# Where the column means of the first MLP weight are made and subtracted: first attention and its end, or five visits of the second attention

## The chip, the cores and the metric

One core of one Trainium2 chip runs the whole program. The metric is the device time of one execution in microseconds, the median of several; less is better. All arithmetic of matmuls is fp32, apart from the bucket masks in bf16.

## What is computed

The reference chains a hashed attention and an FNet block. With batch 4, 8 heads, sequence 768 and head size 64:

```python
mask = q_bucket[:, :, :, None] == k_bucket[:, :, None, :]
scores = np.where(mask, scale * np.matmul(q, k.transpose(0, 1, 3, 2)), -1e9)
attn = softmax(scores)                       # rows, with + 1e-9 below
x = (attn @ v) laid out as (B, S, H*D)       # (4, 768, 512)
mixed = np.real(fft(fft(x, axis=1), axis=2))
u = x + mixed
un = (u - mean(u)) / np.sqrt(var(u) + 1e-6)  # over the last axis
out = u + np.maximum(un @ w_ch1, 0.0) @ w_ch2
```

`w_ch1` is 512 x 2048 and `w_ch2` 2048 x 512; both arrive as 64-bit floats and are narrowed to fp32 on the core. Because `(u - mean(u)) @ w1` equals `u @ (w1 - column mean of w1)`, the kernel takes the mean out of the weight instead of out of every row: each column of `w1` has its mean over the 512 inputs subtracted once. The change is about when this is done.

## The kernel before

The batches run one after the other. `attention(b)` (from line 999) goes through 4 pairs of heads, each with 6 chunks of 128 keys: 24 steps, after each of which it yields. A step makes scores on TensorE (L909, with mask matmuls L898 for the first pairs), takes the exponential on ScalarE (L922), masks on VectorE for later pairs (L936), sums keys on VectorE (`acc`, L1041), and multiplies with v on TensorE (`oo`, L947). The exponentials have two buffers `pk`; one becomes free when its sum has been made. Beside the attention of batch b runs a second piece of work, advanced by `next(other)` between the steps: beside the first attention `weights1` (the conversion of `w1`), beside the later ones `mix(b-1)`, which is the Fourier mixing of the batch before (`cs` L1162, `A` and `B` L1191, update of x L1205) and then its MLP as Strassen products (`mlp7`: `h_p` L1471 and `o` L1350). With b = 1 also `w2` is converted on the way.

`w1` lies in SBUF as 4 row blocks by 2048 columns. `average(f)` (L659) makes the mean of 512 columns in two parts. First four matmuls with a 128 x 32 matrix of ones, one for each row block, into four 32-row bands of one PSUM bank `ws` (L664), and a ScalarE copy of that bank to the SBUF tile `part` (L669); then, after a yield, one 128 x 128 matmul with a matrix of 1/(32*512), which leaves the mean in every row of another bank, `wm` (L672). `centre(f, avg)` (L675) subtracts it from the four row blocks on VectorE (L678), 512 columns at a time. The tag `u`, which holds `part`, has two buffers; the PSUM tag `ps`, from which `ws` and `wm` come and outside the first and last stage the banks of the mixing step, has two too.

Before the change, blocks 0 and 512 are averaged and centred within `weights1`, after their fourth conversion, in the first attention. Blocks 1024 and 1536 are averaged at the end of the first attention (L1593 to L1599), their means copied to two SBUF tiles `mean` by ScalarE, and subtracted at the second step of the second attention (L1612 to L1614).

Two things set the order. Everything of the first attention and the averages at its end stands in a block whose order on all engines is that of the text (L1578). After it a planner orders each engine's instructions at compile time: among those that its cost model holds ready, the one that comes first in the text. `in_turn()` (L684) puts what it encloses behind the last recorded instruction of ScalarE and of VectorE on their queues. Centred weights are first read by `quarters` (L1257, VectorE sums L1264 to L1267 and stores `ad` of L1269 and L1270, issued by SP), which prepares the Strassen operands; `quarters(f)` reads columns f*128 and (f+8)*128. SP also issues all loads of q, k and v (L562, L568, L576).

Of the kernel before, what the change touches and what calls it, by code (L numbers as in the profile page):

```python
# [11 lines left out]
F32 = mybir.dt.float32  # L12
# [8 lines left out]
P = 128  # L21
# [3 lines left out]
DFF = 4 * DM  # L25
# [5 lines left out]
NDC = DM // P  # L31
GTT = 2
GT = GTT * P
WC = 512
# [451 lines left out]
def _main(  # L486
# [13 lines left out]
    nc = tc.nc  # L500
# [13 lines left out]
    def wt(shape, dtype, tag, name, bufs=2):  # L514
        return work.tile(shape, dtype, tag=tag, name=name, bufs=bufs)
# [4 lines left out]
    def pt(shape, name):  # L520

        turn[0] += 1
        if roomy[0] and turn[0] % 2:
            if turn[0] % 4 == 1:
                return ps_o.tile(shape, F32, tag="o", name=name)
            return ps_sc.tile(shape, F32, tag="sc", name=name)
        return ps_1.tile(shape, F32, tag="ps", name=name)
# [89 lines left out]
    mean = const.tile([P, P], F32, tag="mean", name="mean")  # L617
# [41 lines left out]
    def average(f):  # L659


        ps = pt([P, WC], f"ws{f}")
        for c in range(NDC):
            nc.tensor.matmul(  # L664
                ps[32 * c : 32 * c + 32, :], ones, w1[:, c, f : f + WC],
                start=True, stop=True,
            )
        part = wt([P, WC], F32, "u", f"part{f}", 2)
        nc.scalar.copy(part, ps)  # L669
        yield  # L670
        ps = pt([P, WC], f"wm{f}")
        nc.tensor.matmul(ps, mean, part, start=True, stop=True)  # L672
        yield ps

    def centre(f, avg):  # L675
        for c in range(NDC):
            w = w1[:, c, f : f + WC]
            nc.vector.tensor_tensor(w, w, avg, op=ALU.subtract)  # L678

    ET = mybir.EngineType  # L680
    done_by = {}

    @contextmanager
    def in_turn():  # L684

        with ExitStack() as st:
            for ins in done_by.values():
                st.enter_context(tc.issue_after(ins.ins))
            yield
# [32 lines left out]
    def weights1():  # L722
        slices = [
            (w1[:, c, f : f + WC], moe_w_ch1[c * P : (c + 1) * P, f : f + WC])
            for f in range(0, DFF, WC)
            for c in range(NDC)
        ]
        zt = wt([P, 3, 2 * WC], F32, "z", "zraw1", 1)
        ft = wt([P, 12, WC], F32, "F", "fraw", 1)
        raws = [zt[:, i] for i in range(3)] + [  # L730
            ft[:, i : i + 2].rearrange("p i w -> p (i w)") for i in range(0, 8, 2)
        ]
        arrival = Arrival(slices, raws, 0, nc.sync)
        for i in range(arrival.depth):
            arrival.fetch(i)
            if i == 2:
                load(1)
        yield
        half = None
        for i in range(len(slices)):  # L740
            arrival.convert(i, ft[:, 8 + i % 4].bitcast(I32))
            yield
            if half:
                centre(half[0], next(half[1]))
                half = None
            if i % NDC == NDC - 1:


                f = i // NDC * WC
                if f < DFF // 2:  # L750
                    half = f, average(f)
                    next(half[1])


    xs = {}
# [164 lines left out]
    def weights(pk, g, ps):  # L920

        done_by[ET.Activation] = nc.scalar.activation(  # L922
            pk[:, g, :, 0:HALF], ps[:, :, 0:HALF], AF.Exp, scale=SCALE
        )

    def weigh(n, c, pss):
# [6 lines left out]
        if kb is not None:  # L933
            for h in range(2):
                w = pk[:, :, h, 0:HALF]
                done_by[ET.DVE] = nc.vector.scalar_tensor_tensor(  # L936
                    w, qb[:, h].rearrange("p (g s) -> p g s", g=2), kb[:, h, c : c + 1], w,
# [61 lines left out]
    def attention(b):  # L999
# [14 lines left out]
        for t in range(NPAIR):  # L1014
# [12 lines left out]
            def tally(c, pk, sums):  # L1027
# [10 lines left out]
                else:  # L1038

                    for g in (0, 1) if b == 0 else (slice(0, 2),):  # L1040
                        done_by[ET.DVE] = nc.vector.tensor_tensor(  # L1041
                            acc[:, g], (first if c == 1 else acc)[:, g], new[:, g],
# [102 lines left out]
    def mix(b):  # L1145
# [8 lines left out]
        for par in range(2):  # L1154
            for t in range(NT // 2):
# [12 lines left out]
                for k in kinds:  # L1168
                    done_by[ET.Activation] = nc.scalar.copy(
                        f[:, k, k : hd + 1 - k],  # L1170
# [14 lines left out]
        for j in range(NDC):  # L1185
# [10 lines left out]
            for ps, op in (pa, ALU.add), (pb, ALU.subtract):  # L1196
                for i in range(2):
# [4 lines left out]
                    else:  # L1202
                        f = ps[:, HW : HALF + 1]
                        f = bass.AP(f.tensor, f.offset, [f.ap[0], [HW, 2], [-1, HW]])
                    done_by[ET.DVE] = nc.vector.tensor_tensor(  # L1205
                        u, u, f, op=op if (j < 2) ^ i else ALU.add
# [206 lines left out]
    def mlp7(b):  # L1413
# [66 lines left out]
        def relu(h):  # L1480
# [3 lines left out]
            else:  # L1484
                done_by[ET.Activation] = nc.scalar.activation(h, h, AF.Relu)  # L1485

# [77 lines left out]
    def after(n, one, two):  # L1564

        for i, _ in enumerate(one):
            if i >= n and (i - n) % 2 == 0:
                next(two, None)
            yield
        for _ in two:  # L1570
            pass

    other = weights1()
    next(other)

    with tc.manual_schedule(engines={ET.PE, ET.DVE, ET.Activation, ET.Pool, ET.SP}):  # L1578
        for _ in prepare(0):
            pass  # L1580
        roomy[0] = False
        for i, _ in enumerate(attention(0)):
            if i == 2 * NT - 1:
                nc.sync.dma_start(ch, cn["ch"].ap())
                nc.sync.dma_start(sq, cn["sq"].ap())
            if i % 5 < 4:
                next(other, None)
        for _ in other:
            pass
        pwf = wt([P, 2, P], F32, "ef", "pwf", 1)  # L1590
        nc.sync.dma_start(pwf, cn["pw"].ap())
        nc.scalar.copy(pw, pwf)
        means = []  # L1593
        late = [(f, average(f)) for f in range(DFF // 2, DFF, WC)]
        for _, avg in late:
            next(avg)
        for f, avg in late:
            means.append((f, wt([P, WC], F32, "u", f"mean{f}", 2)))
            nc.scalar.copy(means[-1][1], next(avg))  # L1599
    for b in range(B):  # L1600
        if b > 0:

            wait = 0
            if b == 1:
                next(other)
                next(other)
                wait = 2
            steps, done = NPAIR * NT - wait, 2 if b == 1 else 0  # L1610
            for i, _ in enumerate(attention(b), 1):
                if b == 1 and i == 2:  # L1612
                    for f, avg in means:
                        centre(f, avg)  # L1614
                while done * steps < (MIX - LEFT) * (i - wait):
                    next(other)
                    done += 1
        if b == B - 1:
            roomy[0] = True

            ms = const.tile([P, 3], F32, tag="ms", name="ms")
            nc.vector.tensor_reduce(ms[:, 0:2], norms, axis=AX.X, op=ALU.max)
            nc.vector.tensor_reduce(ms[:, 2:3], strange, axis=AX.X, op=ALU.max)
            ps = pt([1, 3, P], "norms_t")
            for io in range(3):
                nc.tensor.transpose(ps[:, io, :], ms[:, io : io + 1], ident)
            mt = const.tile([1, 5], F32, tag="mt", name="mt")
            nc.vector.tensor_reduce(mt[:, 0:3], ps, axis=AX.X, op=ALU.max)  # L1630
            nc.vector.tensor_tensor(mt[:, 3:4], mt[:, 0:1], mt[:, 1:2], op=ALU.mult)
            nc.vector.tensor_scalar(
                mt[:, 4:5], mt[:, 3:4], (SAFE / SCALE / 2) ** 2, None, op0=ALU.is_gt
            )
            fl = const.tile([1, 1], I32, tag="fl", name="fl")
            nc.vector.scalar_tensor_tensor(
                fl, mt[:, 2:3], 0.0, mt[:, 4:5], op0=ALU.is_gt, op1=ALU.max
            )
            large = nc.values_load(fl[0:1, 0:1], min_val=0, max_val=1)
        for _ in other:  # L1640
            pass
        other = mix(b)
        if b == 0:
            zt2 = wt([P, 3, 2 * WC], F32, "z", "zraw2", 1)
            arrival2 = weights2()
            other = after(NT, other, islice(arrival2, HF + 2))
# [6 lines left out]
def kernel(tc, *args):  # L1653

    cn = {n: tc.nc.inline_tensor(a, name="k_" + n) for n, a in _consts().items()}
    with ExitStack() as ctx:
        large = _main(ctx, tc, *args, cn)
    with tc.If(large > 0, preferred_fallthrough_block=True):
        _any_scores(tc, *args, cn)
# [34 lines left out]
```

## Time and profile before

| what | us |
|---|---|
| median of 3 runs | 1074.12 |
| lowest and highest | 1073.25, 1074.61 |
| the profiled execution | 1074.1 |
| its span, first to last instruction | 1072.3 |
| TensorE, weight loads, VectorE, ScalarE busy | 1033.3, 632.4, 779.6, 489.2 |
| `ws` matmuls: first and last start | 33.8, 115.2 |
| `wm` matmuls: first and last start | 39.4, 118.4 |
| subtractions from `wm`: first and last start, median of one | 40.6, 66.0, 0.680 |
| subtractions from `mean`: first and last start, median of one | 119.7, 130.6, 0.680 |
| copies to `mean`: two, median of one | 0.604 |

In the lines of the profile, a row of the chain of work has its start, its length and what ran: the engine, the tile that it writes, and the line of the code; x4 is the number of instructions merged. PE is TensorE (PEld its weight loads), DVE VectorE, ACT ScalarE, POOL GpSimd, SP the engine that issues DMAs; a q behind a name means the engine's queue. The scores matmuls of the second attention begin at 115.7 us, its mixing matmuls at 126.3 us; the third attention's begin at 394.94 us (`cs`).

### The profile page before, as it was taken

The numbers are of one execution on the slowest core, as the hardware profiler recorded it, in microseconds if no ns is written. First come the engines' busy times: TensorE is split into PE (matmuls) and PEld (weight loads), VectorE is DVE, ScalarE is ACT, GpSimd is POOL, SyncE is SP. The second block draws the span as 40 slices with busy tenths as digits, with TensorE's granted clock in tenths as the row PEclk, the third lists the DMA queues.
The fourth block names the chain that finished last, engine by engine and source line by source line (L and its number), as shares of the span: only waits on it lengthen the run. The fifth ranks groups of instructions, "written<-read, shape, count | busy, mean of one in ns | idle before, by whom it ended". The sixth has DMA issues, their size and how long they took to land.

```text
span 1072.3 us, 14129 instructions
## 1 busy us (share of the span) xinstructions
PE 1033.3 (96%) x4965; PEld 632.4 (59%) x4965; DVE 779.6 (73%) x1326; ACT 489.2 (46%) x993; POOL 59.6 (6%) x132
## 2 busy tenths in 40 slices
PE   7999899999999999999999999999999999999996
PEld 3333364457644676546665675555675579668575
DVE  5789969996799967877758877767857885644353
ACT  7888564761386323455236315354325512440420
POOL 0000000011000020100000020010000012200000
PEclk9999999999999999999999999999999999999999
DMA  8754551470154451223072242322042204223301
GB/s 207 200 143 85 112 136 45 135 233 1 35 153 150 136 194 36 45 67 81 12 200 74 66 123 88 59 64 61 15 125 86 64 25 172 65 74 100 117 20 42
DMA packets 175711, 103.13 MB, mean 96 GB/s; under 512 B 129553, under 2 KB 162961, under 8 KB 175633
## 3 DMA queue, kind: packets, MB, share of 16 engines
q1 hardware_dynamic: 169840, 88.65, 30.7%
q0 software_dynamic: 4224, 13.11, 3.9%
q8 instruction: 41, 0.67, 0.3%
q10 hardware_dynamic: 1568, 0.39, 0.2%
q14 instruction: 38, 0.30, 0.1%
HBM read 81.14 MB, written 20.97 MB: 95 GB/s over the span
## 4 chain that ended last, share of the span: by engine, by line
PE 74%; DVE 14%; ACT 5%; issue 2%; DMA 2%; SPq 1%; DVEq 0%; ACTq 0%
PE o L1350 25%; PE h_p L1471 23%; PE oo L947 9%; PE sc L909 8%; PE cs L1162 3%; DVE pk L936 2%; DVE acc L1041 2%; ACT pk L922 2%; PE A L1191 2%; PE B L1191 1%; PE sum L957 1%; DMA kn<-in_k_dram 1%; DVE x L1205 1%; PE bits L838 1%; SPq L576 1%
## 5 line engine op out<-in xcount | busy, mean ns | idle before, releaser
L1350 PE MATMUL o<-w,h 128*128 128x256 f32 x1152 | 258.6, 381 | 0.9 <-DVE w L1362 0.5
L1350 PEld LDWEIGHTS o<-w,h 128*128 128x128 f32 x1152 | 216.7, 190 | 41.6 <-issue 6.4
L922 ACT ACTIVATE pk<-sc 128x768 f32<-128x768 f32 x192 | 147.4, 808 | 78.6 <-PE oo L947 35.5
L1471 PE MATMUL h_p<-x,w 128*128 128x384 f32 x448 | 164.5, 494 | 2.4 <-ACT w L1538 1.7
L936 DVE SCALAR_TENSOR_TENSOR pk<-qb,kb,pk 128x768 f32<-128x768 bf16 x132 | 128.8, 1012 | 39.4 <-ACT pk L922 39.3
L909 PE MATMUL sc<-qt,kt 64*128 64x384 f32 x768 | 153.6, 503 | 1.6 <-ACT pk L922 1.4
L947 PE MATMUL oo<-pk,vn 128*64 128x385 f32 (+1 forms) x768 | 146.2, 495 | 1.5 <-DVE pk L936 1.3
L1471 PEld LDWEIGHTS h_p<-x,w 128*128 128x128 f32 x448 | 81.9, 190 | 68.3 <-issue 9.3
L1471 PE MATMUL h_p<-w 128*128 128x384 f32 x288 | 105.9, 489 | 0.0
L1041 DVE TENSOR_TENSOR acc<-acc,pk 128x1536 f32<-128x1536 f32 (+1 forms) x64 | 98.5, 1550 | 5.4 <-ACT pk L922 5.2
L947 PEld LDWEIGHTS oo<-pk,vn 128*64 128x64 f32 x768 | 50.5, 136 | 86.5 <-issue 73.7
L909 PEld LDWEIGHTS sc<-qt,kt 64*128 64x128 f32 x768 | 66.2, 186 | 55.4 <-issue 19.3
L1471 PEld LDWEIGHTS h_p<-w 128*128 128x128 f32 x288 | 53.7, 190 | 38.8 <-issue 1.6
L1362 DVE SCALAR_TENSOR_TENSOR w<-o,rs,w 128x256 f32<-128x256 f32 x56 | 26.6, 480 | 41.6 <-PE o L1350 41.6
L1380 ACT COPY tq<-o 128x256 f32<-128x256 f32 x24 | 8.9, 372 | 104.0 <-PE o L1350 104.0
L1485 ACT ACTIVATE h<-h 128x384 f32<-128x384 f32 x72 | 37.4, 524 | 29.0 <-DVE h L1527 14.0
L1350 PE MATMUL o<-w 128*128 128x256 f32 x176 | 42.2, 383 | 0.3 <-DVE w L1362 0.2
L1522 DVE TENSOR_TENSOR h<-h 128x384 f32<-128x384 f32 x32 | 17.8, 555 | 29.2 <-ACT h L1521 29.1
L1100 POOL DMA_DIRECT2D out_dram<-w x30 | 16.3, 546 | 405.4 <-issue 321.4
L1350 PEld LDWEIGHTS o<-w 128*128 128x128 f32 x176 | 32.9, 190 | 7.6 <-DVE w L1362 1.2
L1396 DVE TENSOR_TENSOR tq<-tq,o 128x256 f32<-128x256 f32 x24 | 10.0, 418 | 36.4 <-PE o L1350 36.4
L1369 ACT COPY tq<-o 128x256 f32<-128x256 f32 x24 | 8.8, 368 | 60.3 <-PE o L1350 60.2
(171 smaller groups left out, 1306.0 us busy)
## 6 DMA issues: line engine op xcount, KB each, us to landing
w<-ad SPq DMA_DIRECT2D x168, 128.0 KB, 2.0
w<-bd SPq DMA_DIRECT2D x42, 512.0 KB, 4.5
zraw<-in_moe_w_ch_dram POOLq DMA_DIRECT2D x16, 512.0 KB, 3.9
bd<-w SPq DMA_DIRECT2D x14, 512.0 KB, 4.4
vn<-in_v_dram SPq DMA_DIRECT2D x32, 192.0 KB, 3.3
qn<-in_q_dram SPq DMA_DIRECT2D x120, 48.0 KB, 2.4
kn<-in_k_dram SPq DMA_DIRECT2D x60, 96.0 KB, 3.1
zraw<-in_moe_w_ch_dram SPq DMA_DIRECT2D x8, 512.0 KB, 6.6
```

The lines of the kernel that those rows point to most:

```text
L909: last[0] = nc.tensor.matmul(ps[:, h, 0:HALF], kt[rows, ks], qt[rows, qs], start=kb is not None or early, stop=not early,)
L922: done_by[ET.Activation] = nc.scalar.activation(pk[:, g, :, 0:HALF], ps[:, :, 0:HALF], AF.Exp, scale=SCALE)
L936: done_by[ET.DVE] = nc.vector.scalar_tensor_tensor(w, qb[:, h].rearrange("p (g s) -> p g s", g=2), kb[:, h, c : c + 1], w, op0=ALU.is_equa ...
L947: oo = nc.tensor.matmul(oos[g][h * D : (h + 1) * D, 0:w], nat["v", n][:, (2 * c + h) * D : (2 * c + h + 1) * D], pk[:, g, h, 0:w], start=( ...
L1041: done_by[ET.DVE] = nc.vector.tensor_tensor(acc[:, g], (first if c == 1 else acc)[:, g], new[:, g], op=ALU.add,)
L1162: nc.tensor.matmul(ps[:, pc + 2 * lo : pc + 2 * hi - 1 : 2], z[:, cp, pc, par, t * P : (t + 1) * P], ch[:, cp, pc, lo:hi], start=(cp == 0) ...
L1191: nc.tensor.matmul(ps[:, cols], F[:, par, k, t, j * P : (j + 1) * P], sq[:, t, k, cols], start=(t == 0), stop=(t == 1),)
L1350: nc.tensor.matmul(ps, a[:, r], right7[i][:, r], start=start and r == 0, stop=r == HF // 2 - 1, skip_group_check=not start,)
L1362: nc.vector.scalar_tensor_tensor(t[:, cols], src, r, t[:, cols], op0=ALU.mult, op1=ALU.add)
L1471: nc.tensor.matmul(ps, left[:, k], right[i][:, k], start=start and k == 0, stop=k == 1, skip_group_check=not start,)
L1485: done_by[ET.Activation] = nc.scalar.activation(h, h, AF.Relu)
L1522: done_by[ET.DVE] = nc.vector.tensor_tensor(c22, c21, c22, op=ALU.add)
```

## The change

A generator `centrings` is advanced once after each step of the second attention, inside `in_turn()` and ahead of that step's share of `other`. Its first three calls do nothing. The fourth makes `ws` and `part` of block 0; the fifth makes `wm` of block 0, subtracts it and makes `ws` and `part` of block 512; and so on to the eighth, which makes `wm` of block 1536 and subtracts it. All subtractions read the mean from PSUM. `weights1` and the end of the first attention have no averages any more, and the tiles `mean` and their copies are gone. By the shares of `other`, the seventh visit is directly ahead of the first `quarters`.

```diff
@@ -677,6 +677,17 @@
+    def centrings(columns, visits):
+
+        for _ in range(visits):
+            yield
+        for f in columns:
+            avg = average(f)
+            next(avg)
+            yield
+            centre(f, next(avg))
+        yield
+
     ET = mybir.EngineType
     done_by = {}
@@ -736,20 +747,9 @@
-        half = None
         for i in range(len(slices)):
             arrival.convert(i, ft[:, 8 + i % 4].bitcast(I32))
             yield
-            if half:
-                centre(half[0], next(half[1]))
-                half = None
-            if i % NDC == NDC - 1:
-
-
-                f = i // NDC * WC
-                if f < DFF // 2:
-                    half = f, average(f)
-                    next(half[1])
@@ -1590,13 +1590,7 @@
         nc.scalar.copy(pw, pwf)
-        means = []
-        late = [(f, average(f)) for f in range(DFF // 2, DFF, WC)]
-        for _, avg in late:
-            next(avg)
-        for f, avg in late:
-            means.append((f, wt([P, WC], F32, "u", f"mean{f}", 2)))
-            nc.scalar.copy(means[-1][1], next(avg))
+    centred = centrings(range(0, DFF, WC), 3)
@@ -1609,9 +1603,9 @@
             for i, _ in enumerate(attention(b), 1):
-                if b == 1 and i == 2:
-                    for f, avg in means:
-                        centre(f, avg)
+                if b == 1:
+                    with in_turn():
+                        next(centred, None)
                 while done * steps < (MIX - LEFT) * (i - wait):
                     next(other)
                     done += 1
```

## The prediction

> **What bounds the kernel now.** I read the busy time first, then the chain of work that ended last, stretch by stretch, because TensorE's busy share alone decides nothing. The page's first part:
>
> ```profile
> PE 1033.3 (96%) x4965; PEld 632.4 (59%) x4965; DVE 779.6 (73%) x1326; ACT 489.2 (46%) x993; POOL 59.6 (6%) x132
> ```
>
> TensorE looks full, yet matmul ends are modelled, so I count its idle time from starts: each matmul record is charged the spacing that it has when packed in the chain (h_p 0.322 us, oo 0.180, sc 0.163, and so on). That gives 982 us of work and 77 us of waiting in the span. The change moves work out of 30-131 us into 131-182 us, so these stretches matter (TensorE waiting by that count; VectorE idle from the gaps between its instructions): 30-70: TensorE waits 4.3; 110-131: 3.8; 131-166: 3.0 (VectorE idle 10.2); 166-182: 5.8 (VectorE 0.0).
>
> The chain in the window 30-50 us, columns start, us, what:
>
> ```profile
> 33.22 0.78 PE sum L957 x8
> 34.01 0.86 PE ws L664 x8
> 34.86 0.27 PE sc L898 x2
> ...
> 40.65 2.38 DVE w L678 x4
> ```
>
> A mean's matmuls and the four subtractions stand on the chain of the first attention. The same happens to the second block: its matmuls and ScalarE copy, from the chain of 10-142 us:
>
> ```profile
> 57.52 0.54 DVE qkb L816
> 58.10 1.11 PE ws L664 x8
> 59.23 0.58 ACT part L669
> ...
> 118.94 0.84 DVE ef L1122
> 119.78 0.60 DVE w L678
> 120.38 0.94 DVE ef L1127 x2
> 121.31 0.60 DVE w L678
> 121.92 1.07 DVE z L1136 x4
> ```
>
> From 100 to 128 us the chain is VectorE nearly throughout, and four late subtractions lie in it before the key sums at 126 us. The next row of the chain after them names a store, but the exponential at 127.83 us waited 5.18 us for those sums, so I follow that wait. From 131 us the chain is TensorE (window 130-184):
>
> ```profile
> 132.64 0.78 PE bits L838 x8
> 133.43 3.08 PE cs L1162 x16
> 136.77 1.09 PE cs L1162 x8
> 137.86 0.85 PE sc L909 x4
> ...
> 164.95 0.83 PE sum L957 x8
> 165.80 0.58 DVE rt L979
> 166.38 1.64 DVE acc L1041
> ```
>
> So the receiving stretch has VectorE room but little TensorE room until 166, and then VectorE sets the pace until 182.
>
> [...] 0.680 us from `wm` in PSUM, 0.680 from `mean` in SBUF. [...] ScalarE sat 4.22 us before `part` at 59.23 with conversions queued behind. [...] eight `ws` records take 0.98 us (33.82 to the next matmul at 34.80), two untiled `wm` records 1.06 us (39.39 to 40.45), 4.3 times as much per record[...]. [...] Each mean takes two of the `ps` banks in turn, the two that the mixing step also uses.
>
> **The change part by part.** Prices: one mean costs TensorE 0.98 + about 1.0 = 2.0 us; ScalarE 0.58; VectorE four subtractions, 2.38 us start to start.
>
> *Removed from the first attention, blocks 0 and 512.* On the chain: 0.86 + 2.38 for the first, 1.11 + 0.58 for the second, together 4.9 us. The second's subtractions are left out, since the chain passes to the queue of loads at 62 us; that queue waits for the conversion which stood behind `part` on ScalarE, so it moves up too. Bounds: 3.0 if loads land no earlier, 6.5 if the second `wm` and some subtractions count.
>
> *Removed at its end, blocks 1024 and 1536.* Ten matmul calls (4.0 us of TensorE), two copies to `part` and two to `mean` (1.07 and 1.08 us of ScalarE) lie beside a full VectorE: nothing by themselves. Eight subtractions: four stand before the sums, 4 x 0.60 = 2.4 us; the other four (128.80 to 131.2) are followed by VectorE idle time, nothing. Bounds 1.5 to 4.8. VectorE goes on to the fold, which is next in its queue. Sum removed: 4.9 + 2.4 = 7.3 us.
>
> *Added.* Visits 4 to 8 of the second attention: 8.0 us of TensorE, 2.3 of ScalarE, 16 subtractions, 9.5 us of VectorE. The visits fall at about 131, 138, 145, 152 and 158 us by the scores matmuls. The first four bring four `ws` and three `wm`, 6.9 us, into the TensorE-bound stretch. They need only `w1`, so they can run where the queue otherwise waits; of its 3.0 us I let them fill 2.5. That leaves 4.4. The last `wm`, 1.0 us, has lower priority than the mixing work of visit 7 and finds the 5.8 us of waiting after 166: nothing. VectorE: 9.5 us against 10.2 us of idle plus the 4.4 us of longer stretch: nothing, as long as the subtractions get into 134-150, where 8.4 of the idle lies; without that cover up to 4.8 us. ScalarE has 15.7 us idle in 131-166: nothing. No run shows this mixture; bounds 1.5 (waiting up to 182 is filled too) to 9.9 (below).
>
> *New waits.* `part` waits for `ws`, with exponentials and F copies queued behind it and scores waiting for those; a subtraction waits for `wm`, with key sums, masks and x updates behind it; `wm` holds a bank until the fourth subtraction, 2.5 us, while cs, A and B want both. They are short if the means run as soon as placed, and are in the bound. The 24 stores of `ad` wait for centred weights: 18 of them took SP 12.6 us before; six that ran at 92 us join them. Loads of q and k for pair 6 are issued from 147 on SP; ScalarE waited for k until 166. I take 0, as SP idles from 138 to 147; up to 3 us in the bound.
>
> *Only the place differs* for the rest: TensorE's total is unchanged, ScalarE's falls by two copies. From 182 us on the work is the same; I take the shift as carried to the end.
>
> Sum: 4.4 - 7.3 = -2.9 us. The profiled execution took 1074.1 us (span 1072.3 plus 1.8 around it), the median is 1074.12: forecast **1071.2 us**.
>
> **The rivals.**
>
> *All filled.* The added matmuls also fill waits after 166, and the cost falls to 1.5: 1074.1 - 7.3 + 1.5 = 1068.3. For it: 5.8 us of waiting there; against it: those waits end on VectorE, which gets more work. With the larger removal end it reaches 1064.
>
> *One for one.* TensorE is the resource of both places (9.7 to 10.2 us of counted work per 10 us in 30-40 and 60-70 too); nothing is filled, 7.3 us go and about 7.3 come: 1074.1. For it: TensorE's total is conserved.
>
> *Slower, by VectorE's place.* The subtractions of visits 7 and 8 (4.8 us) fall into 150-182, where VectorE has 1.8 us idle, ahead of x updates that free the banks of A and B and ahead of the Strassen quarters. Then 6.9 of matmuls with nothing filled, plus 4.8 - 1.8 = 3.0: 9.9 - 7.3 = +2.6, 1076.7; with 3 us of late loads 1080. For it: the chain at 166-174 is VectorE; against it: the 8.4 us of room just before. It decides as soon as the added cost exceeds 7.3: nothing filled and over 0.4 us of subtractions on VectorE's path.
>
> *Not doing what it says* would be a planner that delays all means until the quarters need them at 170; that ends in the slower case.
>
> **How the numbers follow.** Likeliest (1071.2) 0.40, all filled 0.17, one for one 0.15, slower 0.28. About 0.2%, 2.1 us, is what this measurement can tell from no change. The likeliest case's own range, 1068.5 to 1073.5, is faster in 0.28 of its 0.40; all filled adds 0.17, a little of one-for-one 0.01: faster 0.46. Same: 0.12 + 0.14 = 0.26. Slower 0.28. The range takes in most of both outer cases, for the new order of the mixing work after 131 is unshown: 1064.5 to 1079.0.
>
> **What would show it.** Right: the first scores of the second attention some 4 to 5 us earlier, the 131-us point about 7 earlier, no wait of ScalarE before `part` over 2 us, TensorE's waiting in the mixing stretch below before's, and the 182-us point about 3 earlier. Wrong: the first attention shortened by under 3 us; `w L678` on the chain next to `x L1205` or before the quarters; ScalarE's square waiting longer for k; or a shift at 182 us that has gone by the third attention (cs at 394.94 us before).

## The result, and the profile after

| | median of its runs, us | lowest, highest |
|---|---|---|
| before (6 runs) | 1073.86 | 1072.95, 1076.33 |
| after (6 runs) | 1082.57 | 1081.59, 1083.76 |

The ratio is 1.0078 with a 95% interval of 1.0067 to 1.0089: 8.7 us slower, where 2.9 us faster was forecast, and above the range's top of 1079.0. The profiled execution of after took 1083.76 us, with a span of 1082.0.

The busy times again, the page's first part:

```profile
PE 1036.8 (96%) x4965; PEld 633.2 (59%) x4965; DVE 779.7 (72%) x1326; ACT 488.7 (45%) x991; POOL 59.7 (6%) x132
```

As many matmuls and VectorE instructions as before, and VectorE busy within 0.1 us of before (TensorE's 3.5 us more are no added work, since matmul ends are modelled): the 8.7 us are waiting. To find where, I set the same matmul of both traces side by side (the n-th of its kind) and took the difference of their starts. At before's 131.1 us after is 7.1 us early, at the first MLP product (`h_p`, 178.6) it is 4.4 late, at the 33rd MLP product (192.1) 11.7 late, at 271.3 10.4 late, and to the end it stays between 9.8 and 10.4. So everything happens before 206 us, in four stretches.

**The first attention.** The chain of after, 10 to 140 us (start, length, what), has no mean in it until the second attention:

```profile
31.51 0.81 ACT pk L922
...
117.56 1.66 DVE acc L1041
...
125.30 1.76 DVE acc L1041
...
135.19 1.06 PE wm L672 x2
136.25 0.97 PE ws L664 x2
```

What stood at 34.01 (`ws`), 40.65 (subtractions), 58.10 and 119.78 is gone. The removal came as forecast: 4.7 us by the last products of the first attention (before's 109 us), 7.1 at 131.1.

**The mixing stretch, before's 131 to 165 us.** In after, three `ws` and two `wm` run in it, 4.9 us at the prediction's prices; the last two lines above show a pair on the chain. At the `sum` product that ends the stretch, which stands at 164.88 in before, after has lost its whole lead of 7.1 us:

```profile
164.87 0.85 PE L957 MATMUL sum<-acc,ones 128*32 128x384 f32 x8 [0.55 <-DVE x L1205]
```

**VectorE's stretch, 165 to 175 us.** The chain of after, 160 to 175:

```profile
166.48 0.57 DVE w L643
...
167.15 0.59 DVE w L678
167.74 0.67 DVE w L652 x2
168.41 0.21 DVE rr L983
168.62 1.73 DVE w L678 x3
170.35 0.52 DVE x L1205 x2
170.88 0.33 issue
171.20 1.75 DVE acc L1041
```

`wm` of block 1024 ran at 165.80, 14 us later than the prediction had its visit, and its four subtractions stand on VectorE's queue ahead of an update of x and of the key sum `acc`. That sum began at 171.20, where before had it at 166.31. The timeline of after (start, length, what, and in brackets the engine's idle time ahead and who ended it) shows who waits:

```profile
172.98 1.51 ACT L922 ACTIVATE pk<-sc 128x768 f32<-128x768 f32 x2 [2.83 <-DVE acc L1041]
173.85 1.61 PE L909 MATMUL sc<-qt,kt 64*128 64x384 f32 x8 [1.54 <-ACT pk L922]
```

The sum frees a `pk` buffer; the exponential waits for it, and TensorE's scores wait for the exponential.

**The first MLP products, 182 to 206 us.** The same timeline, further on:

```profile
182.51 0.66 PE L1217 MATMUL un<-ident,x 128*128 128x128 f32 x4
...
192.30 1.13 PE L672 MATMUL wm<-part,mean 128*128 128x512 f32 x2 [0.57 <-ACT h L1514]
193.46 0.59 ACT L1218 COPY u<-un 128x512 f32<-128x512 f32 x1 [0.51 <-PE wm L672]
194.10 1.56 PE L1471 MATMUL h_p<-bt,tq 128*128 128x384 f32 x4 [0.68 <-ACT u L1218]
...
196.14 2.47 DVE L678 TENSOR_TENSOR w<-w,wm 128x512 f32<-128x512 f32 x4
196.23 1.56 PE L1471 MATMUL h_p<-x,tq 128*128 128x384 f32 x4 [0.57 <-ACT h L1521]
...
198.35 1.56 PE L1471 MATMUL h_p<-x,tq 128*128 128x384 f32 x4 [0.57 <-ACT h L1530]
```

and the same work in the timeline of before:

```profile
178.76 0.59 ACT L1218 COPY u<-un 128x512 f32<-128x512 f32 x1 [5.35 <-PE un L1217]
...
186.99 2.74 PE L1471 MATMUL h_p<-x,tq 128*128 128x384 f32 x8
```

The transposes `un` fill one of the two `ps` banks. In before their copy to a tile of tag `u` runs as soon as they are done; in after it comes at 193.46, just behind the last `wm`. A tile `u` is not to be had, since `part` of block 1536 holds one of the two until that `wm` has read it. Then `wm`'s own bank stays taken until VectorE has made its four subtractions at 196.14 to 198.6. For 16 us (182.5 to 198.6) the MLP has one bank: a product (1.56), ScalarE's copy (0.5), the next product, 2.13 us apart at 194.10, 196.23 and 198.35. Before packs two products in 2.74, and the one behind them starts 2.58 us after the first (189.57), so that a product takes 1.29: the second bank is worth 0.84 us a product here, and that is what a mean parked in it takes away.

### The profile page after: what moved, and what is told of

It is laid out like the page before. It is cut to its first block, busy times and chain, and to the rows that moved or that the text cites. A ratio compares the mean times of both kernels' runs of the same rounds, so it can differ in the third digit from the quotient of the medians.

```text
span 1082.0 us, 14129 instructions
## 1 busy us (share of the span) xinstructions
PE 1036.8 (96%) x4965; PEld 633.2 (59%) x4965; DVE 779.7 (72%) x1326; ACT 488.7 (45%) x991; POOL 59.7 (6%) x132
## 4 chain that ended last, share of the span: by engine, by line
PE 72%; DVE 14%; ACT 7%; issue 3%; SPq 2%; DMA 2%; DVEq 0%; ACTq 0%
PE o L1350 25%; PE h_p L1471 23%; PE oo L947 8%; PE sc L909 8%; PE cs L1162 3%; ACT pk L922 2%; DVE pk L936 2%; DVE acc L1041 2%; PE A L1191 2%; DMA kn<-in_k_dram 1%; PE B L1191 1%; SPq L576 1%; DVE x L1205 1%; ACT zraw L654 1%; PE bits L838 1%
```

## The experiments

Two theories, formed from the two traces. **Place:** the means of blocks 0 and 512 are harmless; of the other two, the subtractions hold up VectorE's queue at 167 us, and `part` and `wm` hold a tile and a bank of the MLP from 182 on. **Rival, one for one:** a mean costs its TensorE time wherever it stands, and nothing else matters. The table gives each run's median and ratio to before (runs of the same chip; before's median was 1073.47 to 1074.38 in these rounds), and from its trace how late the same matmul starts against before: at the end of the first attention, at the first MLP product, and beyond the means. In e3, e7, e8 and e11 the planner has put the first MLP product ahead of `oo` products that precede it in before, so that their figures at 178.6 look better than the work done by then is.

| run | median | ratio [95% interval] | at 131.1 | at 178.6 | at 271.3 |
|---|---|---|---|---|---|
| after | 1082.57 | 1.0078 [1.0067, 1.0089] | -7.1 | +4.4 | +10.4 |
| e1_none | 1065.43 | 0.9913 [0.9885, 0.9942] | -7.3 | -7.3 | -7.4 |
| e2_part_s1s | 1080.37 | 1.0057 [1.0040, 1.0075] | -7.4 | +3.6 | +6.1 |
| e3_visits1 | 1075.07 | 1.0010 [1.0001, 1.0018] | -5.9 | -1.8 | +0.3 |
| e4_s1s_sbuf | 1077.77 | 1.0036 [1.0025, 1.0047] | -7.9 | +3.7 | +4.5 |
| e5_visits2 | 1079.66 | 1.0039 [1.0026, 1.0052] | -7.4 | +4.5 | +5.9 |
| e6_visits0 | 1074.15 | 0.9999 [0.9989, 1.0009] | -2.5 | +0.5 | +0.5 |
| e7_no_sub | 1074.36 | 0.9992 [0.9980, 1.0003] | -7.2 | -2.7 | +1.7 |
| e8_sub_only | 1068.88 | 0.9937 [0.9912, 0.9962] | -6.9 | -6.8 | -3.7 |
| e9_pool_sums | 1080.26 | 1.0054 [1.0033, 1.0075] | +3.0 | +6.6 | +7.7 |
| e10_pool_half | 1081.41 | 1.0077 [1.0050, 1.0103] | +1.8 | +3.6 | +4.0 |
| e11_no_sub_1024 | 1081.01 | 1.0067 [1.0047, 1.0087] | -7.9 | -0.3 | +5.5 |
| e12_no_sub_1536 | 1079.07 | 1.0049 [1.0030, 1.0068] | -7.8 | +3.9 | +6.3 |

### No means at all (e1_none)

```diff
-                if b == 1:
-                    with in_turn():
-                        next(centred, None)
```

> Leaves out the column means altogether (nothing is averaged or subtracted from the first MLP weight), all else as after the change. Both theories: what the removal alone is worth, as the prediction's sum had it, 7.3 us, so about 1066.5 us; the trace of the changed kernel shows 7.1 us at 131 us. A value of 1070 or more would say that the removal's gain is lost again later by itself, in the new order of the second attention.

1065.43 us: all means of after taken together cost 17.1 us, and leaving out those of before is worth 8.6. The trace stays 7.3 early from 131 us to the end of the stretch, so the gain of the removal does not fade by itself; what takes it away is added later.

### The last block's `part` in a tile of its own (e2_part_s1s)

```diff
-        part = wt([P, WC], F32, "u", f"part{f}", 2)
+        part = s1s[0].rearrange("p r n -> p (r n)") if f == DFF - WC else wt([P, WC], F32, "u", f"part{f}", 2)
```

> As after the change, but the last block's copy `part` lies in an unused slice of w2's tile (s1s[0]) and not in a buffer of tag u, so the copy of the transposed tile u (across, T=5) need not wait for the last mean's matmul. Theory placement (the loss comes from the last two visits: a bank held by the transposes until the buffer u is free, a bank held by the mean, and subtractions ahead of the key sum at 166-171 us): 3 to 5 us below the changed kernel, 1078 to 1080. Theory work (20 matmul calls and 16 subtractions cost what they take wherever they stand in the second attention): no change, 1082 to 1083.

`s1s[0]` is a slice of w2 that is empty until the MLP. Up to the first MLP product little changes (+3.6 for +4.4); beyond the means 4.3 us are won back in the trace, 2.2 in the median, which is just over the 1078 to 1080 that I expected. The timeline shows why: the copy runs when the transposes are done, 11 us earlier, and `wm` at 189.26 for 192.30.

```profile
182.32 0.59 ACT L1218 COPY u<-un 128x512 f32<-128x512 f32 x1 [5.92 <-PE un L1217]
...
189.26 1.02 PE L672 MATMUL wm<-w,mean 128*128 128x512 f32 x2
```

### The last block's mean out of its bank, too (e4_s1s_sbuf)

```diff
@@ on top of e2_part_s1s
-        yield ps
+        yield (nc.scalar.copy(part, ps), part)[1] if f == DFF - WC else ps
```

> As the kernel before it (part of the last block in s1s[0]), and the last block's mean is copied by ScalarE from its bank back to that slice, the subtractions reading SBUF, so that the bank is free after one copy and not after the fourth subtraction. Theory placement: the serial products between 192 and 199 us in the changed kernel get their second bank back, 5 to 8 us below the changed kernel, 1075 to 1078, and 2 to 3 below the run with the other buffer alone. Theory work: 1082 to 1083.

ScalarE copies the mean to SBUF, which frees the bank, and the subtractions read the copy: 1077.77, another 2.6 us less, 1.6 by the trace. Both holds, of the tile and of the bank, are real. From the first MLP product to 271 us after loses 6.0 us (4.4 to 10.4), e2 2.5 and e4 0.8. One for one has no room for this, since the matmuls are the same and ScalarE has more to do.

### One, two and three visits earlier (e5_visits2, e3_visits1, e6_visits0)

```diff
-    centred = centrings(range(0, DFF, WC), 3)
+    centred = centrings(range(0, DFF, WC), 2)   # e5; 1 in e3, 0 in e6
```

> As after the change, but two idle visits in place of three: means at visits 3 to 7, so that the last mean stands in the text ahead of the step in which the MLP begins. Theory placement (the loss beyond the price of the matmuls is made by the last two visits meeting the first MLP products): most of it goes, 1075 to 1078. Theory load (VectorE's stretch after 160 us is the limit, whatever the text's order): 1079 to 1082.

> As after the change, but the first three idle visits are one: means are made and subtracted at visits 2 to 6, so that all are done before the seventh step, where the MLP begins. Theory placement: the 3 us for the first means stay, perhaps 6 with VectorE full before 128 us, and the 14 us of the last two visits go: 1070 to 1074. Theory work: 1080 to 1083, since the same instructions are in the same attention.

> As after the change, but no idle visit: means at visits 1 to 5, from 112 us on, where VectorE was full in the kernel before. Theory one-for-one (the matmuls cost their 8 us wherever TensorE is the limit, the subtractions are hidden): 1073 to 1075, as with one idle visit. If subtractions in the VectorE stretch before 128 us cost as in the kernel before: 1076 to 1079.

With 2, the last block is now where block 1024 was in after: its `wm` at 165.8, its subtractions at 167.1 to 170.4, and the key sum at 171.2 as in after. The MLP part is gone (+4.5 at the first product, +4.3 still at before's 202 us) and VectorE's part is not. The median, 1079.66, lies over what the place theory expected and in the range of the other expectation, which puts the loss down to VectorE's load. The trace is a poor measure beyond that: its execution is the longest of e5's twelve, 1082.15 us at a mean granted clock of 0.993 (after's has 0.998), and how much of the table's +5.9 goes with the clock was not shown. With 1 and 0, all subtractions are over by 149.4 and 144.4 us, the key sum runs at 166.3 and 166.8 as in before, and the time is that of before (1.0010, a little over what I expected, and 0.9999); so where the means stand in the text does matter. There the rival's rule fits: e6's means cost 8.7 us over e1_none, close to the 8.0 us of their matmuls, and before's cost 8.6; no run takes matmuls and subtractions apart at these visits.

### Means without subtractions, and subtractions without means (e7_no_sub, e8_sub_only)

e7 leaves out the sixteen subtractions, so the weight is not centred; e8 leaves out the means' matmuls and copies and subtracts a constant instead.

```diff
@@ e7
-            centre(f, next(avg))
+            next(avg)
@@ e8
-            avg = average(f)
-            next(avg)
             yield
-            centre(f, next(avg))
+            centre(f, mhalf.broadcast_to([P, WC]))
```

> Leaves out the 16 subtractions of the column means (the means are made and not used), all else as after the change. Tells TensorE's share from VectorE's. Theory placement: the wait for the tag u stays (4 us), the bank held by the last mean and the subtractions ahead of the key sum go, so about 1065.4 + 8 + 4 = 1077. If the subtractions make nearly all of the 17 us: 1068 to 1071. If the matmuls do: 1080 or more.

> Leaves out all matmuls and copies of the means; the 16 subtractions stand at the same visits and take a constant (so that not the column mean is subtracted). Theory placement: the subtractions of the first two visits are hidden, those of the last two partly not: 1067 to 1071. If VectorE's load makes nearly all of the loss: 1075 or more.

Against e1_none, matmuls and copies alone cost 8.9 us, subtractions alone 3.4, both together 17.1. So some 4.8 us come only where both are there; I put them down to subtractions that wait for matmuls and hold their banks meanwhile, as the traces of after, e2 and e4 show it. I had expected e7 to stay at about 1077: the subtractions cost more than I had given them. e8's 1068.88 lies where I expected it. In e7's trace the key sum is back at its place (166.61):

```profile
148.97 0.89 PE L1191 MATMUL B<-sq,F 128*128 128x193 f32 x4 [1.42 <-ACT part L669]
...
165.18 0.85 PE L957 MATMUL sum<-acc,ones 128*32 128x384 f32 x8
...
166.61 1.72 DVE L1041 TENSOR_TENSOR acc<-pk,pk 128x1536 f32<-128x1536 f32 x1
...
175.89 0.81 PE L1471 MATMUL h_p<-x,w 128*128 128x384 f32 x2
...
178.08 1.50 PE L947 MATMUL oo<-pk,vn 128*64 128x385 f32 x4 [1.39 <-DVE pk L936]
```

The `sum` at 165.18 is 7.6 us behind that of e1_none (157.56), and the matmuls of the 15 us ahead of it are as late. So the first five pieces, 4.9 us of matmuls, cost 7.6: they filled no waiting, and TensorE sat 1.42 us more at 148.97 until ScalarE had made a `part`. At 271 us e7 is 9.1 behind e1_none, so the last three pieces, 3.0 us, cost 1.5. Here the rival is right and the place theory is not: the means of the first two blocks aren't harmless, their matmuls cost what they take and more. (The first MLP product is no measure in e7: it is 2.7 us early, but the `oo` at 178.08 stands ahead of it in before, at 175.04, and is 3.0 late.)

### The subtractions of one block left out (e11_no_sub_1024, e12_no_sub_1536)

Each leaves four subtractions out, so one block is not centred.

```diff
-            centre(f, next(avg))
+            ps = next(avg)
+            if f != 2 * WC:      # 3 * WC in e12
+                centre(f, ps)
```

> The changed kernel without the four subtractions of block 1024 (so that block is not centred). Place theory: these four are what holds the key sum back at 166 to 171 us, so the sum starts at about 167 and the first MLP product at 178 to 180 instead of 183.0; the later loss by the held banks stays: 1077 to 1079. If all subtractions cost alike (8.2 us for sixteen): 2 us less, 1080.5.

> The changed kernel without the four subtractions of block 1536 (so that block is not centred). Place theory: nothing changes up to the first MLP product at 183.0 us; then the bank of the last wm comes free when its matmul ends instead of at 198.6, so two or three products pack again, 1 to 2.5 us less: 1080 to 1081.5. If the bank's hold is nothing beside the buffer's, within 0.5 us of the changed kernel (1082.6). If all subtractions cost alike: 1080.5.

In e11's timeline the sum and the first product moved as expected (the product in part because it now precedes `oo` products), and in e12's the products pack again as soon as the last `wm` is done. Behind the edit, the line numbers of these two kernels are higher by two:

```profile
166.76 1.75 DVE L1043 TENSOR_TENSOR acc<-pk,pk 128x1536 f32<-128x1536 f32 x1
...
178.28 1.46 PE L1473 MATMUL h_p<-x,w 128*128 128x384 f32 x4
```

```profile
191.77 1.12 PE L672 MATMUL wm<-part,mean 128*128 128x512 f32 x2 [0.57 <-ACT h L1516]
192.95 1.56 PE L1473 MATMUL h_p<-bt,tq 128*128 128x384 f32 x4
194.35 2.74 PE L1473 MATMUL h_p<-x,tq 128*128 128x384 f32 x8
```

By the traces at 271 us, block 1024's subtractions cost 4.9 us and block 1536's 4.1, together 9.0, and all sixteen cost 8.7 (after against e7): if the parts add, nothing is left for the subtractions of the first two blocks. The medians bear out e12 (3.5 us less, more than expected). They do not bear out e11: its profiled execution took 1078.61, inside the expectation, but the other three 1079.89 to 1082.16, and the median, 1081.01, lies nearer to the 1080.5 of "all subtractions cost alike". So the whole time can't confirm the 4.9 us; what the longer executions did no trace shows. What else speaks for them is e5 against e3: key sum at 171.2 or at 166.3, the time 3 us longer by the ratios and 4.6 by the medians.

### The sums on GpSimd (e9_pool_sums, e10_pool_half)

Tried as a version that might beat both: the sum of the four row blocks leaves TensorE and ScalarE, `ws` and `part` are gone, and the visits are those of e6. e10 has also two of the four subtractions on GpSimd, from a copy of the mean in SBUF. The main lines of e9's edit, cut:

```diff
+    def sums(f):        # in the first attention, after each fourth conversion
+        t = total(f)    # a slice of w2 that is still empty
+        for c in range(1, NDC):
+            nc.gpsimd.tensor_tensor(
+                t, w1[:, 0, f : f + WC] if c == 1 else t, w1[:, c, f : f + WC], op=ALU.add
+            )
@@ average(f)
+        nc.tensor.matmul(ps, mean, total(f), start=True, stop=True)
```

> The four row blocks of each 512 columns are summed by GpSimd (twelve additions of 128 x 512, behind every fourth conversion of w1, in the first attention) into slices of w2 that are still empty; TensorE makes only the 128 x 128 product with 1/512, ScalarE no copy, and product and subtractions stand on visits 1 to 5 of the second attention. Place theory: at these visits a mean costs what its TensorE work is, so four ws of 0.98 us less than the run with visits 1 to 5 (1074.2): 1070.3, range 1069 to 1072. Rival, TensorE work is hidden and VectorE is what counts: no gain, 1073.5 to 1075. A second rival, GpSimd's additions slow VectorE while they run beside it in the VectorE-bound first attention: 1075 or more, with the first scores of the second attention later than before.

> As the run with the sums on GpSimd, and ScalarE copies each mean to SBUF, and GpSimd makes the subtractions from two of the four row blocks. If VectorE's eight subtractions of 0.60 us are on the path at visits 1 to 5, some 1 to 3 us less than with the sums alone: 1067.5 to 1069.5. If they are covered there (the subtractions alone cost 3.4 us at visits 4 to 8), within 1 us of it. If GpSimd is so slow that the first quarters wait for its blocks, or holds VectorE up, over it.

Both are slower than before. At before's 109 us, in the first attention, e9 is 1.6 us late where e6 is 4.8 early, and by then no mean has run on TensorE in either. The second rival of the expectation is what happened, though its sign showed only against e6 (first scores of the second attention: e9 0.5 us early, e6 7.4). Two lines of e9's timeline show it (L1045 is the key sum there):

```profile
43.10 2.91 DVE L1045 TENSOR_TENSOR acc<-pk,pk 128x768 f32<-128x768 f32 x2
...
43.26 1.93 POOL L667 TENSOR_TENSOR w<-w 128x512 f32<-128x512 f32 x1 [7.94 <-DVE w L649]
```

Two key sums that take 1.82 us together in before take 2.91 beside the addition; of the two one takes 0.95, as in e6, and the other 2.04. VectorE's busy time is 790.8 us, 11 more than before. e10's profiled execution took 1077.19 and its others up to 1084.65; that it isn't faster than before is all I take from it.

## Why the prediction was wrong

**Right: what is removed.** 7.3 us were forecast and e1_none and after are 7.3 and 7.1 early at 131 us; 8.6 in e1's median. The first attention gave 4.8 and 4.7 of it, for 4.9 forecast. The sign "first scores of the second attention some 4 to 5 us earlier" came out as 7.3, since the late averages stood ahead of them on TensorE, too.

**Failed: "of its 3.0 us I let them fill 2.5. That leaves 4.4."** Nothing was filled before 166 us: the five pieces that ran by then, 4.9 us, cost 7.6 (e7 against e1_none at the `sum`). Only the waits after 166 took some of it back, and all matmuls and copies together cost 9.1 us by the traces and 8.9 by the medians, about twice the 4.4. "ScalarE ...: nothing" failed with it in part: its busy time had room, but `part` came late, and TensorE waited 1.42 us for one in e7. ScalarE's own longest wait before `part` was 2.4 us in after, over the 2 us that I had named as a sign.

**Failed: "The last `wm`, 1.0 us, has lower priority than the mixing work of visit 7 and finds the 5.8 us of waiting after 166: nothing."** It ran neither at 158 nor at 166 but at 192.30, and what waits for it isn't TensorE's room but a `u` tile, and behind that a bank. Of the 6.0 us that after loses from the first MLP product on, 3.5 go with the tile (e2) and 1.7 more with the bank (e4); 0.8 are left, about the matmul's own time. By the medians the two are 2.2 and 2.6. They aren't independent: with the tile held but no subtractions on the bank (e12) the loss is 2.4. "From 182 us on the work is the same; I take the shift as carried to the end" failed with this step. The text ahead of the prediction says that the tag `u`, which holds `part`, has two buffers; the prediction never asked who else needs them while `part` has one.

**Failed: "VectorE: ... nothing, as long as the subtractions get into 134-150".** Eight did; the other eight ran at 167.1 to 170.4 and 196.1 to 198.6. All sixteen cost 8.7 us by the traces, and without them the change would have been level with before (e7, 0.9992). The sign named for this case, `w L678` next to `x L1205` on the chain, stands at 168.62 to 170.35. I placed visits 7 and 8 at 152 and 158 us by the scores matmuls. In the traces no mean's matmul runs between 146.6 and 164.9 us in after, e2 or e5, whatever visit it belongs to: a piece that has missed the first window waits some 20 us for the next. Why the planner leaves that gap I didn't test.

**Mis-sized: the slower rival and the bounds.** The rival named the stretch and VectorE's queue, but as what waits it named x updates ("that free the banks of A and B"), where the trace shows the key sum, and it gave the subtractions 3.0 us; they cost 8.7 by the traces, 8.2 by the medians. Four subtractions delay the key sum by 4.4 us (171.20, 166.76 in e11) and not by 2.4, since it also falls behind conversions of w2 and an update of x. And "`wm` holds a bank until the fourth subtraction, 2.5 us" was only weighed against cs, A and B, not against MLP products that need two banks. By traces at 271 us: 9.1 for matmuls and copies, 8.7 for subtractions, less 7.4 for the removal, make 10.4; forecast, 4.4 + 0 - 7.3 = -2.9.

**One for one** (0.15) fits the whole time at visits 1 to 5 and 2 to 6, and in the change itself the matmuls (9.1 us with their waits, for 8.0); it has no term for the subtractions and the holds.

## What to carry to other kernels

Work that is "off the path" still takes buffers: before you move it, list each tile and bank that it holds, until which instruction, and who else draws on the same rotation at that time; here a mean whose last matmul takes 1.0 us cost 6.0 us in the MLP, 5.2 of them by the tile and the bank that it kept. Here a low-priority piece was not hidden but late (at 192.30 us, for a forecast 158), so price such a piece at the place where it will run if it misses the gap you meant for it, and look at its consumers' queue there. When you compare two traces matmul by matmul, see that the neighbours agree: the order may have changed. If a move between two stretches bound by the same engine can at best be one for one, only the risk is left.

## What I had not expected of the hardware

In e9 a GpSimd addition of 128 x 512 takes 1.27 to 1.39 us with no key sum beside it and 1.86 to 1.93 beside a VectorE sum of two SBUF tiles, and that sum goes from 0.95 to as much as 2.05 us. Side by side both are longer, the addition by some 0.6 us and the sum by up to 1.1, which is close to the 1.28 of an addition alone; what makes them so was not shown. So GpSimd was no free engine in a stretch that VectorE bounds: VectorE's busy time of 790.8 us is 11 above before's, with as many instructions (1326).
